# The second matrix product of every tile two slots later, and a new order of the block sums, in a spectral mixing layer with an MLP

## The chip, the cores and the metric

One core of a Trainium2 chip runs the whole program. The metric is device time in microseconds (us) of one execution. Inputs and outputs lie in HBM in float32; matrix products run in float16 with float32 accumulation.

Short names: PE is TensorE (matrix products), PEld its weight loads, DVE is VectorE, ACT is ScalarE, POOL is GpSimd, SP is SyncE, which issues most DMAs. Each of them works through its own queue in order.

## The reference

```python
X = np.fft.rfft(x, axis=1)                    # x: (8, 3008, 256)
Yr = Xr @ w_r - Xi @ w_i + b_r                # 256 x 256 complex mixing
Yi = Xr @ w_i + Xi @ w_r + b_i
Y  = soft-shrink of Yr and Yi by 0.01
y  = np.fft.irfft(Y, n=3008, axis=1)          # (8, 3008, 256)
h  = y.reshape(24064, 256) @ w_in             # w_in: 256 x 2048
out = (s * relu(h)**2 + b) @ w_out            # w_out: 2048 x 256
```

## The kernel before

**Tiles.** The MLP is cut into 48 tiles of up to 512 tokens, numbered 0 to 47 here. Batches 0 and 1 have six "wide" tiles each (0 to 5, 6 to 11), the others five "main" tiles each; the last 14 x 32 tokens of pairs of batches make "tail" tiles of 512 or 384 tokens, put between the batches. Tiles 12, 17, 23, 29, 35 and 41 are the first of batches 2 to 7.

**First stage.** `first_mm(ti, mc)` (L851) is one *slot*: for one of 16 blocks of 128 hidden columns it runs two 128x512 matmuls into half of a two-bank PSUM buffer `psh` (two such buffers). After every odd slot ACT takes the pair out with one relu (`rt`, L871), and either ACT (L881) or DVE (L884) squares it into `gt` (float16). A tile has two `gt` buffers of 8 blocks, q = 0 and q = 1; four of them are in rotation.

**Second stage.** `gt` times `w_out` comes in two forms, both cut into 16 slots of matmuls. `second_mms(ti)` (L922) is the plain form: 64 matmuls of 256 columns into the PSUM banks `psa`, whose results DVE takes out with a scale and a bias (L945). `seven_mms(ti)` (L983) is a Strassen-like form with seven products instead of eight on 2x2 blocks, 112 matmuls of 128 columns, seven in a slot. It is used for tiles 4 to 6, for the last two full tiles ahead of each of the batches 2 to 7 (10, 11, 15, 16, 21, 22, 27, 33, 34, 39) and for 41, 42, 43 and 45. Its blocks of `gt` are called a11, a12, a21, a22, and it needs four operations per half q, all written by `s_op(ti, n, q)` (L965):

- n=1 (DVE, L980): s1 = a21 + a22. 
- n=3 (DVE, L980): a21 = a11 - a21, in place, after n=1.
- n=2 (DVE, L980): a11 = a11 - s1, in place, when product 0 of that half has read a11.
- n=4 (a DMA on POOL's queue that adds, L973): a12 += a11, when product 1 has read a12.

Products 0 and 1 share one PSUM bank, product 2 has the next, 3 and 4 the one after, 5 and 6 the last; outside of the last batch there are two such banks, so product 3 (the matmuls `psa<-T_s,s` in the profile, matmul number 48 of the 112, in slot 6) can't begin until DVE has read products 0 and 1. DVE reads them in `leave(0)` (two adds at L1012, written in slot 4). `leave(1)`, `leave(2)` and `leave(3)` (slots 6, 11 and 15) take the other products out, and `leave(3)` also issues the stores of the tile.

**The work beside it.** A dictionary `plan` puts units of the spectral part at slots, counted over all tiles (`ti * 16 + mc`): `s1_units` (first DFT step, `psf<-x,A_t`, result `u`), `s23_units` (forward step `psf<-F_t,us`, evicted into `xf`, whose two halves DVE sums at L672; the sums' product `psf<-W_t,xf`; the mixing `psf<-W_g,xf`, which DVE adds into `ring` at L699, followed by the shrink at L714 to L716; the inverse step `psf<-ring,T_t`, evicted into `v`), and `s4_units` (last DFT step `psf<-C_t,vs`, evicted into `yt`). They share two PSUM banks, `psf`. `s4_units` of a batch run in the last tile ahead of it (5, 11, 16, 22, 28, 34, 40); `s23_units` of the next batch begin with its first tile (6, 12, 17, 23, 29, 35).

**What sets the order.** The main loop (L1126 on) goes through the tiles and slots: the planned units of the slot, then `first_mm`, then one slot of the second stage of the tile before. In slots 10 and 11 of a seven-product tile it writes the sums n=1 and n=3 of the half q = 0 between `first_mm` and the second stage. Two things stand between the loop and the queues. `evac` and `act_first` choose ACT or DVE for each eviction and each square by running totals of the two engines' planned load, which PE's planned time brings up to date. And the layer that records the kernel orders the instructions of each engine once more by its own model of what is ready, so that neighbours can change places.

The lines of the second stage's plan:

```python
for at, n, q in ((2, 2, 0), (2, 1, 1), (2, 4, 0), (3, 3, 1), (4, 2, 1), (5, 4, 1)):   # L1060
    at += alone and at > 3                     # alone: the last batch
    slots[at].append(lambda n=n, q=q: s_op(ti, n, q))
for at, group in ((4 + alone, 0), (6, 1), (11, 2), (15, 3)):
    slots[at].append(lambda group=group: leave(group))
```

Of the kernel before, what the change touches and what calls it, by code (L numbers as in the profile page):

```python
# [96 lines left out]
def kernel(  # L97
# [19 lines left out]
    MC = DFF // P  # L117
# [694 lines left out]
    def width(tl):  # L812
        return 16 * tl[3] if tl[0] == "wide" else tl[3]
# [37 lines left out]
    def first_mm(ti, mc):  # L851
        tl = tiles[ti]
        w = width(tl)
        if mc % 2 == 0:
            hold_h["ps"] = two_banks()
        ps = hold_h["ps"]
        for dc in range(DC):
            o = ps[:, mc % 2, 0:w]
            r = rhs_of(tl, dc)
            if tl[0] == "main":  # L860
                o = o.rearrange("p (n m) -> p n m", m=16)
            if tl[0] == "wide":
                o = o.rearrange("p (n m) -> p n m", n=HW)
            matmul(
                o, w_in_t[dc][:, mc * P : (mc + 1) * P], r,
                start=(dc == 0), stop=(dc == DC - 1),
            )
        if mc % 2 == 0:
            return
        rt = rpool.tile([P, 2, 512], F32, name="rt", tag="rt")  # L870
        nc.scalar.activation(out=rt[:, :, 0:w], in_=ps[:, :, 0:w], func=AF.Relu)  # L871
        q, g = divmod(mc // 2, 4)
        if g == 0:
            gts[(ti, q)] = gpool.tile([P, 2, 2, 4, 2 * P], F16, name="gt", tag="gt")
        gt = gt_view(ti, q)[g]
        rr = rt[:, :, 0:w]
        if halves(ti):
            rr = rr.rearrange("p k (i t) -> p k i t", i=2)
        work("act", 0.07 + w / 600.0)
        if act_first(pe["now"], 0.09 + w / 600.0, 0.07 + w / 480.0):  # L880
            nc.scalar.activation(out=gt, in_=rr, func=AF.Square)  # L881
            work("act", 0.09 + w / 600.0)
        else:
            last_square[0] = nc.vector.tensor_tensor(out=gt, in0=rr, in1=rr, op=ALU.mult)  # L884
            work("dve", 0.07 + w / 480.0)
# [36 lines left out]
    def second_mms(ti):  # L922

        tl = tiles[ti]
        size = sub_size(tl)
        nsub = -(-tl[3] * (16 if tl[0] == "wide" else 1) // size)
        hold = {}

        def mm(sub, mc):

            alone = ti == len(tiles) - 1 and sub >= 2
            h = 0 if alone else sub % 2
            if h == 0 and mc == 0:
                hold["ps"] = sum_bank(ti).rearrange("p (h e) -> p h e", h=2)
            ps = hold["ps"]
            matmul(
                ps[0:size, h, :],
                lhs_of(ti, mc, sub),
                w_out_t[:, mc, :],
                start=(mc == 0), stop=(mc == MC - 1),  # L940
            )
            if mc == MC - 1 and (alone or h == 1 or sub == nsub - 1):
                k = h + 1
                ost = opool.tile([P, 2, D], F32, name="ost", tag="ost")
                nc.vector.scalar_tensor_tensor(  # L945
                    out=ost[0:size, 0:k], in0=ps[0:size, 0:k], scalar=s_bc[0:size],
                    in1=bias_bc[0:size].unsqueeze(1).to_broadcast([size, k, D]), op0=ALU.mult, op1=ALU.add,
                )
                work("dve", 0.13 + 0.27 * k)
                for i in range(k):  # L950
                    store(tl, sub - k + 1 + i, ost[:, i, :])

        units = [lambda s=s, m=m: mm(s, m) for s in range(nsub) for m in range(MC)]
        per_slot = -(-len(units) // MC)
        return [units[i * per_slot : (i + 1) * per_slot] for i in range(MC)]
# [27 lines left out]
    def seven_mms(ti):  # L983
# [73 lines left out]
        slots = [[] for _ in range(MC)]  # L1057
        for at, what in enumerate(order):
            slots[at // 7].append(lambda w=what: mm(*w))
        for at, n, q in ((2, 2, 0), (2, 1, 1), (2, 4, 0), (3, 3, 1), (4, 2, 1), (5, 4, 1)):  # L1060
            at += alone and at > 3
            slots[at].append(lambda n=n, q=q: s_op(ti, n, q))
        for at, group in ((4 + alone, 0), (6, 1), (11, 2), (15, 3)):
# [3 lines left out]
    def seven(ti):  # L1067
        if ti >= len(tiles) - 2 or not halves(ti):
            return False
        firsts = [mark[b] // MC for b in range(2, B)]  # L1070
        return (
            ti >= firsts[-1] or 4 <= ti < 7 or any(m - 2 <= ti < m for m in firsts)
        )

    plan = {}
# [32 lines left out]
    for b in range(2, B):  # L1108
        s0, s1, s2 = mark[b - 2], mark[b - 1], mark[b]
        p = s1 - s0  # L1110
        units, take_rows = s1_units(b)
# [4 lines left out]
        units, take_half = s23_units(b)  # L1116
# [7 lines left out]
                )  # L1124

    ti_n = len(tiles)  # L1126
    for ti in range(ti_n + 1):
        nxt = [[]] * MC
        if ti:
            nxt = seven_mms(ti - 1) if seven(ti - 1) else second_mms(ti - 1)  # L1130
        for mc in range(MC):
            if ti < ti_n:
                for u in plan.pop(ti * MC + mc, []):
                    u()
                first_mm(ti, mc)
                if mc in (10, 11) and seven(ti):
                    s_op(ti, 1 if mc == 10 else 3, 0)
            for u in nxt[mc]:
                u()
    assert not plan  # L1140


# [28 lines left out]
```

## Time and profile before

| | |
|---|---|
| median of 3 runs | 838.71 us (838.18 to 838.87) |
| the profiled execution | 838.19 us, its span 836.4 us |
| PE busy | 824.2 us, 99% of the span, 7470 matmuls |
| PE weight loads busy | 598.7 us, 72% |
| DVE busy | 698.8 us, 84%, 1061 instructions |
| ACT busy | 712.2 us, 85%, 953 instructions |
| POOL busy | 79.8 us, 10% |
| granted TensorE clock | 1.000 (mean) |
| DMA | 126 GB/s on average |

The span runs from the first to the last instruction of the profiled execution; 1.8 us of its time lie outside of the span. A busy share says how much of the span an engine had an instruction in work. The views used below are the groups of instructions with what ended the idle time ahead of them, the table of who waited for whom, and the timeline, whose rows give start, duration, engine, line, operation, what is written and read, shapes and count. The duration of a row covers the start-up of an instruction too; neighbours overlap a little, so the step from one start to the next is what an instruction costs its queue.

### The profile page before, as it was taken

Reading aid. Unit: us, or ns where it says so; the run is one execution under the profiler, and the core shown is the slowest. Engines: PE = TensorE matmul, PEld = TensorE weight load, DVE = VectorE, ACT = ScalarE, POOL = GpSimd, SP = SyncE. Lnnn points to the kernel's source line nnn. Section 1 sums busy time; section 2 is a strip of 40 time slices with the busy share of each in tenths; the row PEclk is TensorE's granted clock in tenths of the full one; section 3 lists DMA queues with packets and bytes.
Section 4 is the critical chain, followed back from the end, with each engine's and each line's share of the span. In section 5 each row is a group of like instructions: output and inputs, shape, how many; then the busy total and the mean of one; then the engine's idle time right before and its main releaser. Section 6 shows DMA issues by size and latency. Waiting matters only on the chain.

```text
span 836.4 us, 19090 instructions
## 1 busy us (share of the span) xinstructions
PE 824.2 (99%) x7470; PEld 598.7 (72%) x7470; DVE 698.8 (84%) x1061; ACT 712.2 (85%) x953; POOL 79.8 (10%) x106
## 2 busy tenths in 40 slices
PE   8999999999999999999999999999999999999997
PEld 7857767777677767777677776777767777767765
DVE  5988989978898888877888788787889878889885
ACT  5998988998899989988899888988879888788882
POOL 4550001100011001100010000100001000001000
PEclk9999999999999999999999999999999999999999
DMA  8954578345873378534772258713565133513321
GB/s 201 183 150 103 120 181 213 64 96 132 199 185 65 98 181 198 126 88 116 192 190 65 81 131 206 180 47 97 127 177 138 48 97 90 140 45 76 72 66 61
DMA packets 115516, 105.04 MB, mean 126 GB/s; under 512 B 12646, under 2 KB 100714, under 8 KB 114082
## 3 DMA queue, kind: packets, MB, share of 16 engines
q1 hardware_dynamic: 102498, 80.55, 34.0%
q0 software_dynamic: 12928, 23.27, 17.6%
q8 instruction: 58, 0.95, 0.5%
q14 instruction: 32, 0.26, 0.1%
HBM read 53.52 MB, written 46.66 MB: 120 GB/s over the span
## 4 chain that ended last, share of the span: by engine, by line
PE 81%; DVE 8%; ACT 5%; DMA 3%; issue 2%; POOL 0%; SPq 0%; DVEq 0%; ACTq 0%; POOLq 0%
PE psh L175 33%; PE psa L175 30%; PE psf L175 17%; ACT rt L871 2%; DVE gt L884 2%; DVE gt L980 1%; DMA ring<-ring 1%; DMA x<-in_x_dram 1%; PE psm L175 1%; ACT gt L881 1%; DVE s L980 1%; DVE ost L1012 1%; ACT u L187 1%; DMA vd<-v 0%; DVE zz L1012 0%
## 5 line engine op out<-in xcount | busy, mean ns | idle before, releaser
L871 ACT ACTIVATE rt<-psh 128x1024 f32<-128x1024 f32 (+2 forms) x384 | 387.0, 1009 | 67.4 <-PE psh L175 65.2
L175 PEld LDWEIGHTS <-gt 128*128 128x128 f16 (+1 forms) x3568 | 303.7, 101 | 171.1 <-DVE gt L884 0.5
L175 PE MATMUL psh<-yt,w_in 128*128 128x512 f16 (+1 forms) x1344 | 396.5, 378 | 0.1
L884 DVE TENSOR_TENSOR gt<-rt 128x1024 f16<-128x1024 f32 (+2 forms) x254 | 304.9, 1204 | 88.6 <-ACT rt L871 86.8
L175 PE MATMUL psa<-w_out_t,gt 128*128 128x256 f16 (+3 forms) x2512 | 333.1, 258 | 0.0
L175 PEld LDWEIGHTS <-w_in 128*128 128x128 f16 x1536 | 137.3, 98 | 25.9 <-issue 3.2
L881 ACT ACTIVATE gt<-rt 128x1024 f16<-128x1024 f32 (+2 forms) x130 | 134.8, 1037 | 3.2
L187 ACT CAST u<-psf 96x512 f16<-96x512 f32 x96 | 55.7, 581 | 9.3 <-PE psf L175 8.6
L175 PE MATMUL psa<-T_s,gt 128*128 128x128 f16 (+1 forms) x752 | 63.5, 219 | 0.0
L699 DVE TENSOR_TENSOR ring<-psf,s 128x512 f16<-128x512 f32 x84 | 57.6, 685 | 4.2 <-PE psf L175 3.1
L187 ACT CAST v<-psf 128x512 f16<-128x512 f32 x82 | 47.5, 582 | 14.2 <-PE psf L175 13.3
L973 POOL DMA_DIRECT2D gt<-gt x34 | 31.1, 916 | 262.3 <-PE psh L175 86.3
L234 POOL DMA_DIRECT2D x<-in_x_dram x36 | 19.3, 540 | 386.3 <-PE psf L175 337.7
L175 PEld LDWEIGHTS <-xf 128*128 128x128 f16 x504 | 47.4, 98 | 7.2 <-DVE xf L672 1.7
L175 PE MATMUL psh<-tail,w_in 128*128 128x512 f16 (+1 forms) x192 | 52.1, 352 | 0.0
L175 PE MATMUL psf<-W_g,xf 128*128 128x256 f16 x336 | 50.4, 272 | 0.0
L945 DVE SCALAR_TENSOR_TENSOR ost<-psa,s_bc,bias_bc 128x512 f32<-128x512 f32 (+2 forms) x59 | 43.0, 730 | 4.5 <-PE psa L175 2.3
L187 ACT CAST yt<-psf 128x470 f16<-128x470 f32 (+2 forms) x84 | 43.2, 534 | 3.4 <-PE psf L175 2.2
L187 ACT CAST xf<-psf 128x512 f16<-128x512 f32 x67 | 39.1, 584 | 4.3 <-PE psf L175 4.1
L175 PE MATMUL psf<-x,A_t 94*96 94x512 f16 x102 | 38.9, 382 | 1.7 <-ACT yt L187 0.3
L175 PE MATMUL psf<-C_t,vs 96*128 96x94 f16 (+1 forms) x484 | 37.9, 205 | 0.0
L1012 DVE SCALAR_TENSOR_TENSOR ost<-psa,s_bc,zz 128x256 f32<-128x256 f32 (+1 forms) x64 | 28.8, 479 | 5.4 <-PE psa L175 3.6
(118 smaller groups left out, 758.2 us busy)
## 6 DMA issues: line engine op xcount, KB each, us to landing
out_dram<-ost SPq DMA_DIRECT2D x152, 128.0 KB
ud<-u SPq DMA_DIRECT2D x56, 192.0 KB
us<-ud SPq DMA_DIRECT2D x28, 384.0 KB
vd<-v SPq DMA_DIRECT2D x42, 256.0 KB
vs<-vd SPq DMA_DIRECT2D x14, 768.0 KB
x<-in_x_dram POOLq DMA_DIRECT2D x28, 376.0 KB, 6.5
ring<-ring SPq DMA_DIRECT2D x280, 32.0 KB
gt<-gt POOLq DMA_DIRECT2D x30, 256.0 KB, 4.6
```

The costliest lines, as they stand in the source:

```text
L175: return nc.tensor.matmul(out, lhs, rhs, **how)
L187: return None, nc.scalar.copy(out=dst, in_=src)
L234: nc.gpsimd.dma_start(out=t[0:N1, i * w : (i + 1) * w], in_=xv[:, c * XCH * D + i * w : c * XCH * D + (i + 1) * w],)
L699: nc.vector.tensor_tensor(out=ring[0][:, i % 4], in0=ps, in1=hold[i // 2][:, i % 2].unsqueeze(1).to_broadcast([P, 2, D]), op=ALU.add,)
L871: nc.scalar.activation(out=rt[:, :, 0:w], in_=ps[:, :, 0:w], func=AF.Relu)
L881: nc.scalar.activation(out=gt, in_=rr, func=AF.Square)
L884: last_square[0] = nc.vector.tensor_tensor(out=gt, in0=rr, in1=rr, op=ALU.mult)
L945: nc.vector.scalar_tensor_tensor(out=ost[0:size, 0:k], in0=ps[0:size, 0:k], scalar=s_bc[0:size], in1=bias_bc[0:size].unsqueeze(1).to_broad ...
L973: nc.gpsimd.dma_start(out=a12, in_=a11, accum_op=ALU.add)
L980: nc.vector.tensor_tensor(out=out, in0=a, in1=b, op=op)
L1012: nc.vector.scalar_tensor_tensor(out=out, in0=of, scalar=s_bc[0:size], in1=other, op0=ALU.mult, op1=ALU.add)
```

## The change

The second stage of a tile is written two slots later against the first stages: its 16 slots now lie in slots 2 to 15 of the next tile and slots 0 and 1 of the one after. All that is written with it moves along: the plain form's evictions, `leave(0)` to `leave(3)`, the stores and the adding DMAs. The planned spectral units keep their places. The sums n=1 and n=3 of q = 0 move from slots 10 and 11 to slots 12 and 13, and are written behind the second stage's matmuls of the slot instead of ahead of them.

Within the second stage of a seven-product tile, n=1 of q = 1 moves from slot 2 to slot 1, n=3 of q = 1 from slot 3 to slot 2, ahead of n=2 of q = 0, which stays in slot 2. The other sums, the adding DMAs and the four `leave` groups keep their slots relative to the matmuls.

No matmul, weight load, sum or transfer is added or removed by the diff itself.

```diff
-        for at, n, q in ((2, 2, 0), (2, 1, 1), (2, 4, 0), (3, 3, 1), (4, 2, 1), (5, 4, 1)):
+        for at, n, q in ((1, 1, 1), (2, 3, 1), (2, 2, 0), (2, 4, 0), (4, 2, 1), (5, 4, 1)):
...
     ti_n = len(tiles)
-    for ti in range(ti_n + 1):
-        nxt = [[]] * MC
-        if ti:
-            nxt = seven_mms(ti - 1) if seven(ti - 1) else second_mms(ti - 1)
-        for mc in range(MC):
-            if ti < ti_n:
-                for u in plan.pop(ti * MC + mc, []):
-                    u()
-                first_mm(ti, mc)
-                if mc in (10, 11) and seven(ti):
-                    s_op(ti, 1 if mc == 10 else 3, 0)
-            for u in nxt[mc]:
+    LAG = 2
+    behind = {}
+    for at in range((ti_n + 1) * MC + LAG):
+        ti, mc = divmod(at, MC)
+        if ti < ti_n:
+            for u in plan.pop(at, []):
                 u()
+            first_mm(ti, mc)
+        if 0 < ti <= ti_n and mc == 0:
+            mms = seven_mms(ti - 1) if seven(ti - 1) else second_mms(ti - 1)
+            for k, units in enumerate(mms):
+                behind[at + LAG + k] = units
+        for u in behind.pop(at, []):
+            u()
+        if ti < ti_n and mc in (12, 13) and seven(ti):
+            s_op(ti, 1 if mc == 12 else 3, 0)
+    assert not behind
     assert not plan
```

## The prediction

> **What bounds the kernel now.** I read the page's busy times first, then who waited for whom, then the timeline around each place where PE's starts leave a hole.
>
> ```profile
> PE 824.2 (99%) x7470; PEld 598.7 (72%) x7470; DVE 698.8 (84%) x1061; ACT 712.2 (85%) x953; POOL 79.8 (10%) x106
> ```
>
> PE sets the end. Taking each start-to-start step of PE against the step of the same matmul undisturbed (0.216 us for 512 columns, 0.109 for 256, 0.056 for 128), some 9.1 us lie in holes over 60 ns each behind 46 us, where the first stages begin; 7.9 us of them behind 83 us. A change of order can win or lose only there. The Trainium skill (Perfetto Trace Analysis, Identifying the Most-Contended Engine) calls matmul busy time a bad measure and wants MFU and LDWEIGHTS busy: by its LDWEIGHTS share, 72%, 28% of the span would look open. The gapless starts in the rows here bear out the 99%; no other sentence uses this.
>
> The holes that the change aims at are those ahead of product 3, which needs the bank of products 0 and 1:
>
> ```profile
> PE psa L175 <- DVE ost L1012: 1.4, 4, 0.6
> L175 PE MATMUL psa<-T_s,s 128*128 128x128 f16 x176 | 16.9, 219 | 1.6 <-DVE ost L1012 1.4
> ```
>
> By starts they are seven: 0.39 (tile 5), 0.74 (7), 0.31 (11), 0.19 (22), 0.44 (28), 0.19 (34), 0.44 (40), 2.70 us in all. Tile 40, DVE and then PE:
>
> ```profile
> 721.89 1.22 DVE L884 TENSOR_TENSOR gt<-rt 128x1024 f16<-128x1024 f32 x1
> 723.02 0.68 DVE L980 TENSOR_TENSOR gt<-gt,s 128x1024 f16<-128x1024 f16 x1
> 723.62 0.95 DVE L884 TENSOR_TENSOR gt<-rt 128x768 f16<-128x768 f32 x1
> 724.49 0.68 DVE L980 TENSOR_TENSOR s<-gt 128x1024 f16<-128x1024 f16 x1
> 725.21 0.69 DVE L980 TENSOR_TENSOR gt<-gt 128x1024 f16<-128x1024 f16 x1
> 726.00 0.69 DVE L980 TENSOR_TENSOR gt<-gt,s 128x1024 f16<-128x1024 f16 x1
> 726.61 0.48 DVE L1012 SCALAR_TENSOR_TENSOR zz<-psa,s_bc,bias_bc 128x256 f32<-128x256 f32 x1
> 727.13 0.48 DVE L1012 SCALAR_TENSOR_TENSOR ost<-psa,s_bc,zz 128x256 f32<-128x256 f32 x1
> ```
>
> ```profile
> 726.89 0.50 PE L175 MATMUL psa<-T_s,gt 128*128 128x128 f16 x6
> 727.67 0.23 PE L175 MATMUL psa<-T_s,s 128*128 128x128 f16 x1 [0.28 <-DVE ost L1012]
> ```
>
> DVE goes without a gap from the square of slot 15 to the second add of `leave(0)`; PE follows 0.06 later. Steps to carry on: square 1.14 (0.87 at 384 tokens, 1.07 at 480), sum 0.60, add 0.40 to 0.50, and from other rows 0.67 for L945, 0.60 for L699, 0.21 for L672, 0.56 for a `yt` eviction; on ACT relu then square 1.06, square then relu 0.97.
>
> The second place is the start of a batch, tile 23 (it begins at 437.40):
>
> ```profile
> 438.54 1.23 DVE L884 TENSOR_TENSOR gt<-rt 128x1024 f16<-128x1024 f32 x1
> 439.68 0.48 DVE L1012 SCALAR_TENSOR_TENSOR ost<-psa,s_bc,zz 128x256 f32<-128x256 f32 x1
> ...
> 442.08 0.28 DVE L672 TENSOR_TENSOR xf<-xf 128x256 f16<-128x256 f16 x1
> ```
>
> ```profile
> 441.96 0.85 PE L175 MATMUL psf<-W_t,xf 128*128 128x256 f16 x4
> ```
>
> The four `W_t` matmuls take 0.85 instead of 0.60: 0.24 of waiting for the second `xf` sum. At product 3 there is no hole here.
>
> The third is ACT in tile 25, where `v` waits behind a square and holds a `psf` bank; PE loses 0.28:
>
> ```profile
> 473.51 1.02 ACT L871 ACTIVATE rt<-psh 128x1024 f32<-128x1024 f32 x1 [0.96 <-PE psh L175]
> 474.57 1.06 ACT L881 ACTIVATE gt<-rt 128x1024 f16<-128x1024 f32 x1
> 475.53 0.57 ACT L187 CAST v<-psf 128x512 f16<-128x512 f32 x1
> ```
>
> **The change part by part.** It adds no matmul. What counts is the built order of the queues (before and after), which I laid beside these durations.
>
> *(a) Product 3 in the tiles with the last DFT step.* Before, the chain on DVE from the square of slot 15 starts some 0.85 us after the tile, when its relu is out. The built order of after has: that square, n=1, square of slot 1, L945 (which moved here with the second stage), square of slot 3 (in tiles 22, 28, 34, 40 it went from ACT to DVE), n=3, n=2 of q = 0, a `yt` eviction, n=2 of q = 1, two adds. Full tiles (16, 22, 34): 1.14+0.60+0.67+1.14+1.14+3x0.60+0.56+0.51+0.48+0.06 = 8.10, ready at 8.97. PE now gets there two slots later: 6.97 (measured, tile 22) plus two slots of 0.43+0.44+0.21, 9.12: no wait, 0.38 won in 22 and 34. Tile 11 likewise (8.77 against 8.89): 0.31 won. Tiles 28 and 40: chain 7.66, ready 8.50, PE at 6.23+1.94 = 8.17: 0.33 left of 0.44, 0.22 won together. Tile 5 has two slots without DFT units: ready 8.77, PE 8.25: 0.52 instead of 0.39, 0.13 lost. Sum -0.78. So two slots more time are mostly eaten by one more square and L945 in the same stretch.
>
> *(b) Tiles 19, 25, 31.* With more load planned on ACT, the square of slot 1 goes to DVE, which has 2.8 us idle there; `v` leaves right behind the relu. Three holes of 0.28 go: -0.85.
>
> *(c) The first tiles of the batches (6, 12, 17, 23, 35).* Here the lag costs. The square of slot 15 goes to ACT (built order: relu, square), and n=1 of q = 1 needs it, yet stands in DVE's queue ahead of `leave(3)`'s adds (now in slot 1), the square of slot 1 and both `xf` sums. Tile 23, from its start: relu of slot 15 -0.2 to 0.85, its square to 1.95, n=1 2.0 to 2.6, add 3.0, square of slot 1 (its relu came behind that square, out at 2.9) to 4.1, two adds 5.0, `xf` sums out at 5.3 and 5.5. DVE idles 1.7 us ahead of n=1. PE wants `W_t` at 4.56, and 0.22 later by a first-stage matmul that the built order puts ahead: a wait of 0.56 instead of 0.24. Same for 35 (+0.32) and 17 (0.18 and 0.10 of holes before: +0.28); tile 12: 0.68 instead of 0.38 (+0.30); tile 6: 0.48 instead of none. Sum +1.70.
>
> Then product 3 in the same tiles: the built order has, between `leave(0)`'s two adds, the L699 add of the mixing product of slot 8, written when product 3 is about to begin. DVE cannot start it before those `W_g` matmuls are through. Tile 23 from `W_t`'s end (443.18 by the above): square of slot 5 ready 446.04, `xf` 446.25, first add 446.7, L699 447.3, second add 447.8; PE, with four `F_t` and two first-stage matmuls put ahead, comes at 447.5: 0.25 to 0.35, I take 0.25 in 17, 23, 35; tile 6 has one matmul less ahead: 0.50; tile 12 has no L699 between: 0. Sum +1.25.
>
> Tile 7, where both stand in one queue with a shrink: `F_t` of slot 4 waits 0.77 for the bank that L699 empties late, later 0.3 more, against 0.74: +0.36.
>
> *(d) Both ends.* Tile 0 already runs without a second stage; two more such slots make `psh` wait about 0.13 for a relu. At the end the last tile has 18 slots of second stage alone, and the 0.19 hole at 826.6 may go. Together 0, within -0.2 and +0.5 (half a relu).
>
> *(e) Moved for nothing, by cover.* Stores and adding DMAs keep their order on SP and POOL. The second adding DMA of a tile lands 3.4 to 4.8 us after issue, some 3 us ahead of product 6, before and after; without this cover its excess would be PE's wait. In tile 24 the 12 tail stores (7.1 us of issuing on SP) stand ahead of the 8 `ring` DMAs (5.9 us) as before; `leave(3)` is ready at about 458.4, when SP falls free at 458.8. Squares of the plain tiles get two slots more, where PE waits for none today: nothing. The other holes (tiles 2, 3, 8, 14, 15: about 3 us) have queues changed in small ways: 0, from -1 to +1.
>
> Sum: -0.78 - 0.85 + 1.70 + 1.25 + 0.36 + 0 = +1.7 us. On the profiled execution: span 836.4 to 838.1, time 838.19 to 839.9. The median of the runs is 0.5 above that execution: 838.7 + 1.7 = **840.4 us**. About 0.2% (1.7 us) is what a measurement of this kernel can tell from no change, so the forecast, slower, lies at that edge.
>
> **The rivals.**
> *R1, the reordering covers it.* The recording layer already moved matmuls ahead of the waits in (c). If these, or a DVE a little faster than my steps, hide product 3's wait (1.25) and half of `W_t`'s (0.85): -0.4, 838.3. For it: DVE idles 16% of the span. Against: in tiles 7 and 12 before, where such moves stand too, 0.74 and 0.38 stayed.
> *R2, faster.* One mechanism: the head of DVE's queue in tiles 6, 12, 17, 23, 35. If the square on ACT is out by 1.4 us after the tile's start instead of 1.95 (ACT free half a us earlier, relu at once), the sums reach PE in time, the old `W_t` holes go too (0.38+0.28+0.24+0.24), and DVE is early enough at product 3. Then -0.78 + 0.36 - 0.85 - 1.14 = -2.4: 836.3. Against it: the relu can't begin ahead of its matmuls.
> *R3, the delay travels.* `leave(3)` late by 0.5 us or more in the five tiles pushes the stores, and behind them on SP the `ring` DMAs, until `T_t` waits: five times 0.5 on top, 842.9. For it: SP's queue is full there (13 us of issues in a row). Against: `ring` has several slots of slack.
> *R4, it does not do what it says:* the recording order undoes the shift and all holes stay: 838.7. The built order, with `leave(0)` two slots later, speaks against it.
>
> **How the numbers follow.** Chances: forecast 0.46, R1 0.20, R2 0.22, R3 0.10, R4 0.02. The forecast's own range is 839.3 to 842.2 (bounds of d, e and of the 0.25); 0.14 of its 0.46 falls under 0.2%. Faster 0.22 (R2); same 0.14 + 0.20 + 0.02 = 0.36; slower 0.32 + 0.10 = 0.42. The range reaches into R2 and R3 until 0.2 is left out: 836.5 to 843.0.
>
> **What would show it.** Right: holes at `T_s,s` gone in 11, 22, 34, smaller in 28 and 40; none at `x,A_t` in 19, 25, 31; in 17, 23, 35 DVE idle over 1.5 us ahead of the first L980, `W_t` waiting some 0.5 and `T_s,s` 0.2 to 0.4; DVE busy up by about 10 us, ACT down by about 8 (14 squares went to DVE, 16 evictions to ACT and 2 to DVE by the built order). Wrong: `W_t` in tile 23 gapless (R2), or `T_t` waiting for `ring` DMAs (R3).

## The result and the profile after

The changed kernel takes 846.38 us (median of 4 runs, 846.07 to 849.36) against 838.44 us for the kernel before in the same runs (837.61 to 838.87): a ratio of the means of 1.0104, with a 95% interval from 1.008 to 1.0128. By the medians it is 7.9 us slower. The forecast was slower by 1.7 us, 840.4 us, with a range up to 843.0; the time lies above the range.

The profiled execution of after takes 846.14 us with a span of 844.4 us, 8.0 us more than before. The busy times of the page:

```profile
PE 826.7 (98%) x7470; PEld 600.1 (71%) x7470; DVE 707.1 (84%) x1061; ACT 705.3 (84%) x953; POOL 81.3 (10%) x106
```

DVE has 8.3 us more work and ACT 6.9 us less (forecast: about 10 and 8); PE has 2.5 us more busy time for the same 7470 matmuls, and its clock is granted at 0.996 on average instead of 1.000 (half of that loss is one stretch in the first 12 us, ahead of the first stages; the other is told below). The table of who waited for whom, PE's rows behind 46 us that matter (total us, times, longest):

```profile
PE psf L175 <- DMA vs<-vd: 3.5, 3, 2.2
...
PE psf L175 <- DVE xf L672: 1.3, 4, 0.4
PE psa L175 <- DVE ost L1012: 1.2, 3, 0.5
PE psa L175 <- DMA gt<-gt: 1.1, 2, 0.8
```

Two of these rows are waits for transfers, `vs<-vd` and the adding DMA `gt<-gt`. Before, this table has neither behind 125 us. The chain that ended last says the same: by engine, in the kernel before

```profile
PE 81%; DVE 8%; ACT 5%; DMA 3%; issue 2%; POOL 0%; SPq 0%; DVEq 0%; ACTq 0%; POOLq 0%
```

and after:

```profile
PE 74%; DMA 11%; DVE 8%; ACT 4%; issue 2%; SPq 1%; POOL 0%; DVEq 0%; POOLq 0%; ACTq 0%
```

Measured as in the prediction, by PE's start-to-start steps over the undisturbed step, the holes add up to 20.8 us before and 28.75 us after, all the 8 us of the span. By the matmul that waits (us; places that hardly differ are left out; the last three columns are experiments told below):

| PE waits at | before | after | loads held | and small adds | before, three edits |
|---|---|---|---|---|---|
| `C_t` (mostly for `vs`) | 0.18 | 4.53 | 0.83 | 1.54 | 1.20 |
| half clock, no wait | 0 | 1.65 | 0 | 0 | 0 |
| product 6 (adding DMA) | 0 | 1.40 | 2.79 | 0 | 0 |
| product 3 (`T_s,s`) | 2.70 | 2.62 | 2.63 | 2.60 | 1.86 |
| `W_t` (`xf` sums) | 1.12 | 2.31 | 2.31 | 2.30 | 1.02 |
| `x,A_t` (`v` eviction) | 2.61 | 1.71 | 1.71 | 1.70 | 1.77 |
| `F_t`, `ring` | 1.36 | 1.36 | 1.35 | 1.53 | 1.31 |
| first 46 us | 9.56 | 9.96 | 10.00 | 9.92 | 9.63 |
| all holes | 20.8 | 28.75 | 24.81 | 22.72 | 20.35 |

The first three rows are new but for 0.18 us and hold 7.4 of the 8.0 us. The row of the first 46 us is not the change's doing: the first 559 matmuls, up to 54 us, stand in the same order in both kernels, and profiles of kernels without the lag differ there by up to 1.7 us. The rows that the prediction worked out are compared with it further below.

**Where `vs` goes late.** SP writes `v` out to the buffer `vd` in HBM (L744) and fetches it back in another layout as `vs` (L755), which `C_t` needs; `u` goes by `ud` to `us` in the same way. SP's queue at the last `vd` write of tile 21, before:

```profile
406.90 1.27 SPq L899 DMA_DIRECT2D out_dram<-ost  x2
409.20 0.38 SPq L744 DMA_DIRECT2D vd<-v  x1
...
411.63 0.79 SPq L755 DMA_DIRECT2D vs<-vd  x2
```

and the x load that GpSimd issues there:

```profile
409.62 0.52 POOL L234 DMA_DIRECT2D x<-in_x_dram  x1 [10.98 <-PE psf L175]
```

The stores go out 2.3 us ahead of `vd`, `vd` goes out 0.42 us ahead of the x load, and 2.43 us later it has landed and `vs` is fetched. After, the order on SP is the same, but the times are not:

```profile
414.11 1.27 SPq L899 DMA_DIRECT2D out_dram<-ost  x2
415.48 0.41 SPq L744 DMA_DIRECT2D vd<-v  x1
...
422.53 0.79 SPq L755 DMA_DIRECT2D vs<-vd  x2
```

```profile
414.89 0.52 POOL L234 DMA_DIRECT2D x<-in_x_dram  x1 [10.97 <-PE psf L175]
```

The stores now wait for an eviction of the second stage (L945, 413.33 to 414.08), and `vd`, whose `v` is out at 414.45, stands behind their two issues (1.27 us). It leaves 0.59 us behind the x load and lands 7.05 us later. What the DMA engines carry in these 8 us (415 to 423) by queue, with packets, MB and the share of 16 engines' time:

```profile
q0 software_dynamic: 112, 0.39, 39.9%
q1 hardware_dynamic: 912, 0.72, 28.6%
```

The 112 packets of GpSimd's queue, the x load's, take more of the engines than the 912 packets of SP's: worked out from these rows, one packet of the load has an engine for 0.46 us, one of SP's for 0.04. The Trainium skill (DMA: Bandwidth & Descriptors, Queues, rings and completion order) says that a DMA engine goes round its queues and serves a whole packet of one before the next; `vd`'s small packets taking turns with the load's large ones would agree with these rows, but no view shows single packets waiting. The same happens in tiles 10 and 27 (8.6 and 6.9 us from `vd` to `vs`, 3.7 and 2.4 before), and PE waits in slot 0 of the next tiles: 2.40 us in tile 11, 0.67 in 22, 0.94 in 28. The longest, on PE's timeline:

```profile
232.37 0.60 PE L175 MATMUL psa<-w_out_t,gt 128*128 128x256 f16 x4
235.21 0.38 PE L175 MATMUL psf<-C_t,vs 96*128 96x94 f16 x5 [2.23 <-DMA vs<-vd]
```

**And what the hole does to the clock.** Busy time in stretches around it, with the granted clock, the DMA share and GB/s in the last columns:

```profile
232.00:236.00 4.00, 1.77 (x17) 1.03 (x15) 1.97 (x3) 1.18 (x2) 0.07 (x1) 1.00 1.03 260
236.00:240.00 4.00, 4.00 (x34) 2.97 (x33) 2.81 (x4) 2.55 (x5) 0.00 (x0) 0.57 0.94 240
```

From 236.4 to 239.8 us PE runs at half clock: matmuls of 480 columns step by 0.40 instead of 0.20. That costs another 1.65 us, for which no row of the waits answers.

**The places that the prediction worked out.** Tile 40, DVE and then PE:

```profile
733.63 1.29 DVE L980 TENSOR_TENSOR gt<-gt,s 128x1024 f16<-128x1024 f16 x2
734.83 0.64 DVE L189 CAST yt<-psf 128x470 f16<-128x470 f32 x1
735.39 0.47 DVE L1012 SCALAR_TENSOR_TENSOR zz<-psa,s_bc,bias_bc 128x256 f32<-128x256 f32 x1
735.90 0.48 DVE L1012 SCALAR_TENSOR_TENSOR ost<-psa,s_bc,zz 128x256 f32<-128x256 f32 x1
```

```profile
735.52 0.37 PE L175 MATMUL psf<-C_t,vs 96*128 96x94 f16 x5
...
736.06 0.50 PE L175 MATMUL psa<-T_s,gt 128*128 128x128 f16 x6
736.44 0.23 PE L175 MATMUL psa<-T_s,s 128*128 128x128 f16 x1
```

DVE's queue is the forecast one, `yt` ahead of the adds. Product 3 no longer waits; 0.28 us of the old 0.44 are now lost at the `C_t` matmul ahead of it (735.52), whose bank the same `yt` eviction empties. Tile 23, DVE and then PE:

```profile
443.95 1.22 DVE L884 TENSOR_TENSOR gt<-rt 128x1024 f16<-128x1024 f32 x1
445.27 0.69 DVE L980 TENSOR_TENSOR s<-gt 128x1024 f16<-128x1024 f16 x1
...
448.19 0.48 DVE L672 TENSOR_TENSOR xf<-xf 128x256 f16<-128x256 f16 x2
...
452.46 0.68 DVE L699 TENSOR_TENSOR ring<-psf,s 128x512 f16<-128x512 f32 x1
453.06 0.47 DVE L1012 SCALAR_TENSOR_TENSOR ost<-psa,s_bc,zz 128x256 f32<-128x256 f32 x1
```

```profile
448.53 0.61 PE L175 MATMUL psf<-W_t,xf 128*128 128x256 f16 x4 [0.30 <-DVE xf L672]
...
453.59 0.62 PE L175 MATMUL psa<-T_s,s 128*128 128x128 f16 x8
```

Tile 23 begins at 443.29: the sum n=1 starts 1.98 us in (forecast 2.0), `W_t` is held 0.46 us (forecast 0.56), and L699 stands ahead of the second add, so that product 3 is held 0.28 us (forecast 0.25). What n=1 stands behind is not the forecast picture, though. The square of slot 15 is on ACT, as forecast:

```profile
443.10 1.02 ACT L871 ACTIVATE rt<-psh 128x1024 f32<-128x1024 f32 x1 [0.35 <-PE psh L175]
444.16 1.06 ACT L881 ACTIVATE gt<-rt 128x1024 f16<-128x1024 f32 x1
```

It ends at 445.21. But DVE does not stand idle for it: it squares slot 13 until 445.16 (the first of the DVE rows above) and has 0.1 us of idle time ahead of n=1, where step (c) had 1.7. Tiles 17 and 35 show the same; ahead of n=1 DVE idles 0.18 us in tile 12 and 0.58 in tile 6. ACT in tile 25:

```profile
479.83 1.02 ACT L871 ACTIVATE rt<-psh 128x1024 f32<-128x1024 f32 x1 [0.96 <-PE psh L175]
481.30 0.59 ACT L187 CAST v<-psf 128x512 f16<-128x512 f32 x1 [0.44 <-PE psf L175]
```

The square between the two is gone from ACT, `v` waits for PE alone, and the hole of 0.28 us is gone.

### The profile page after: what moved, and what is told of

The parts are those of the page before. It is cut to its first block, busy times and chain, and to the rows that moved or that the text cites. A ratio compares the mean times of both kernels' runs of the same rounds, so it can differ in the third digit from the quotient of the medians.

```text
span 844.4 us, 19096 instructions
## 1 busy us (share of the span) xinstructions
PE 826.7 (98%) x7470; PEld 600.1 (71%) x7470; DVE 707.1 (84%) x1061; ACT 705.3 (84%) x953; POOL 81.3 (10%) x106
## 4 chain that ended last, share of the span: by engine, by line
PE 74%; DMA 11%; DVE 8%; ACT 4%; issue 2%; SPq 1%; POOL 0%; DVEq 0%; POOLq 0%; ACTq 0%
PE psh L175 30%; PE psa L175 27%; PE psf L175 16%; DMA vd<-v 3%; DMA vs<-vd 2%; DVE gt L884 2%; DMA gt<-gt 2%; ACT rt L871 2%; DMA ring<-ring 1%; DMA out_dram<-ost 1%; DMA x<-in_x_dram 1%; DVE ost L1012 1%; PE psm L175 1%; DVE ring L699 1%; DMA us<-ud 1%
## 5 line engine op out<-in xcount | busy, mean ns | idle before, releaser
L884 DVE TENSOR_TENSOR gt<-rt 128x1024 f16<-128x1024 f32 (+2 forms) x268 | 321.7, 1205 | 75.2 <-ACT rt L871 75.0
L881 ACT ACTIVATE gt<-rt 128x1024 f16<-128x1024 f32 (+2 forms) x116 | 120.2, 1036 | 2.7
L699 DVE TENSOR_TENSOR ring<-psf,s 128x512 f16<-128x512 f32 x84 | 57.6, 686 | 11.7 <-PE psf L175 10.3
L187 ACT CAST yt<-psf 128x470 f16<-128x470 f32 (+2 forms) x89 | 44.9, 518 | 10.6 <-PE psf L175 9.0
L945 DVE SCALAR_TENSOR_TENSOR ost<-psa,s_bc,bias_bc 128x512 f32<-128x512 f32 (+2 forms) x59 | 43.0, 729 | 8.2 <-PE psa L175 7.9
L187 ACT CAST xf<-psf 128x512 f16<-128x512 f32 x75 | 43.5, 585 | 4.3 <-PE psf L175 4.1
```

Of the source, the lines that this page charges most:

```text
L187: return None, nc.scalar.copy(out=dst, in_=src)
L699: nc.vector.tensor_tensor(out=ring[0][:, i % 4], in0=ps, in1=hold[i // 2][:, i % 2].unsqueeze(1).to_broadcast([P, 2, D]), op=ALU.add,)
L945: nc.vector.scalar_tensor_tensor(out=ost[0:size, 0:k], in0=ps[0:size, 0:k], scalar=s_bc[0:size], in1=bias_bc[0:size].unsqueeze(1).to_broad ...
```

## The experiments

Theory D: the loss is the late last `vd` write, which shares the DMA engines with the x load, so that `vs` comes late. Its rivals: the order of the sums, the lateness of the stores by itself, the DVE queue at the start of a batch, and the adding DMAs. All times are medians of the runs, each beside runs of the kernel before on the same chip (838.5 to 838.9 us).

**The two parts of the change.** The lag alone, with the sums in their old order:

```diff
-        for at, n, q in ((1, 1, 1), (2, 3, 1), (2, 2, 0), (2, 4, 0), (4, 2, 1), (5, 4, 1)):
+        for at, n, q in ((2, 2, 0), (2, 1, 1), (2, 4, 0), (3, 3, 1), (4, 2, 1), (5, 4, 1)):
```

> The lag of two slots alone, the sums of the seven-product tiles in their old order. Theory D (the loss is in the DMA queues: with the lag, the stores of a plain tile go ahead of the last write of vd on SP, that write then shares the DMA engines with the load of the next x, and the last DFT step waits for vs): the same loss as the full change, 845 to 847 us against 838.4, holes ahead of psf<-C_t,vs in slot 0 of tiles 11, 22 and 28. Theory Q (the loss is in DVE's queue at the start of a batch, by the new order of the sums): 840 to 842 us, as the first sum no longer stands so early. Theory S (the new order of the sums is good and hides part of the loss): slower than the full change, 847 to 849.

It takes 845.82 us (843.42 to 849.06), ratio 1.0089 [1.0058, 1.0121]. The other half, the new order of the sums put into the kernel before (the same line the other way round, without the lag):

> The new order of the sums alone, without the lag. Theory D: no loss, 837 to 839 us; no waits for vs; the holes ahead of product 3 (2.7 us in all before) shrink a little, as the first two sums can run while products 0 and 1 are in work, and the x DFT step's holes in tiles 19, 25 and 31 stay. Theory Q: 840 to 841, as n=1 of q = 1 stands ahead of the xf sums here too.

It takes 840.78 us (839.02 to 843.19), ratio 1.0022 [1.001, 1.0034]. The lag carries the loss: with it alone, `vd` to `vs` takes 8.5, 7.1 and 7.0 us in tiles 10, 21 and 27 and the `C_t` holes are 4.84 us. The sums by themselves cost about 2 us, as theory Q had it and not theory D: `W_t` waits 1.97 us instead of 1.12 and product 3 3.10 instead of 2.70. With the lag the order of the sums makes no difference there (`W_t` 2.29 us in the old order, 2.31 in the new).

**Late stores, without the lag.** Before, with each store written two slots later and everything else in place:

```diff
-                    store(tl, sub - k + 1 + i, ost[:, i, :])
+                    put_off(tl, sub - k + 1 + i, ost[:, i, :])
...
+            for what in due.pop(slot[0], []):
+                store(*what)
```

> The kernel before with every store of the output written two slots later and nothing else moved; PE's queue is the same matmul for matmul. Theory D: this alone brings most of the loss, since the stores now stand ahead of the last vd write on SP: that write lands 7 to 9 us after its issue instead of 2.4 to 3.7, holes ahead of psf<-C_t,vs in tiles 11, 22 and 28 of 2 to 4 us in all, with a clock at half for 3.4 us if one of them is over 2 us; 841 to 845 us. Theory Q: no difference, 838 to 839.

It takes 838.87 us (837.25 to 842.23), ratio 1.0003 [0.9989, 1.0016], and `vd` to `vs` stays at 2.35 to 3.8 us in these tiles. But the edit did not make the stores late where it matters. SP's queue in tile 21:

```profile
408.56 1.27 SPq L899 DMA_DIRECT2D out_dram<-ost  x2
410.87 0.38 SPq L744 DMA_DIRECT2D vd<-v  x1
```

Both rows stand 1.7 us later than in the kernel before, as everything does there (1.7 us are lost in the first 46 us of this profile): the order is that of before, the stores go out when their data are ready, and `vd` follows 2.3 us behind them and 0.42 us ahead of the x load. The same holds in tiles 10 and 27. So this run is no test of theory D; the kernels that follow are.

**Stores behind `vd`, with the lag.** After, with the stores one slot later still and held behind the last `vd` write on SP:

```diff
+        with ExitStack() as order_of:
+            if last_vd:
+                order_of.enter_context(tc.issue_after(last_vd[0].ins))
+            for what in due.pop(at, []):
+                store(*what)
```

> The changed kernel with every store written one slot later and held behind the last vd write on SP. Theory D: the vd writes of the tiles 10, 21 and 27 go out 1.3 us earlier and land in 2.4 to 4 us; the holes ahead of psf<-C_t,vs (4.0 us) and the slow clock behind the one of 2.4 us (1.7 us) go: 840 to 841 us. Theory Q: nothing of the loss goes, 845 to 847.

It takes 842.79 us (840.67 to 844.63), ratio 1.0046 [1.0028, 1.0065]: 3.6 us come back, if not all that was expected. `vd` leaves 0.42 us ahead of the x load again, `vd` to `vs` falls to 2.42, 2.4 and 2.4 us, the `C_t` holes to 0.81. But the waits at product 6 grow to 2.99 us, a second transfer that the profile of after only hinted at.

**The x load held, with the lag.** After, with the three loads of the collisions held until the first half of `vs` has landed, by a one-element copy on GpSimd; SP's queue stays as it is:

```diff
-                    lambda b=b, c=c: emit_load_x(b + 1, chunks=range(c, c + 1))
+                    lambda b=b, c=c: emit_load_x(
+                        b + 1,
+                        vs[(b - 1, 0)][0:1, 0, 0:1] if c == 1 and b in (3, 5, 6) else None,
+                        range(c, c + 1),
+                    )
```

> After, with the three x loads that run at the ends of tiles 10, 21 and 27 (chunk 1 of batches 4, 6 and 7) held back until the first half of vs has landed (a 1-element copy on GpSimd waits for it). Nothing else changes: stores still stand ahead of the last vd write, the lag is 2. Theory D (the late vd write shares the DMA engines with the x load's 4 KB packets, so vs lands late and C_t holds PE): vd to vs falls from 7 to 8.6 us to 2.4 to 4 us, the C_t holes from 4.5 us to under 0.8, the clock stays at 1.0: 840 to 842.5 us. Rival (the stores ahead of vd, or SP's own issuing, make vs late): vd to vs stays at 6 us or more and the time at 845 or above.

It takes 842.29 us (841.32 to 844.33), ratio 1.005 [1.0034, 1.0065]: 4.1 us come back. SP's queue in tile 21:

```profile
410.36 1.27 SPq L899 DMA_DIRECT2D out_dram<-ost  x2
411.73 0.41 SPq L744 DMA_DIRECT2D vd<-v  x1
...
415.50 0.79 SPq L755 DMA_DIRECT2D vs<-vd  x2
```

`vd` is as close behind the stores as in after (1.37 us), but without the load beside it lands in 3.77 us instead of 7.05. The half clock is gone too. So the load beside `vd` is most of the delay, 3.3 of 4.6 us. The other 1.3 us, up from the 2.43 of before, remain with the stores right ahead; in tile 33 of after, where no x load runs, `vd` to `vs` takes 3.61 us instead of 2.45 in the same way. What is left of the waits:

```profile
PE psa L175 <- DMA gt<-gt: 2.2, 3, 1.0
PE psf L175 <- DVE xf L672: 1.3, 4, 0.4
PE psa L175 <- DVE ost L1012: 1.2, 3, 0.5
```

**The collision in the kernel before.** No lag; the last `vd` write of the same three batches is held behind the next `ud` write on SP:

```diff
+            def write_behind():
+                with tc.issue_after(last_ud[0].ins):
+                    write()
...
+            if i == H - 1 and b in (2, 4, 5):
+                plan.setdefault(mark[b] - 28, []).insert(0, write_behind)
```

> Before (no lag, old sums), with the last vd write of batches 2, 4 and 5 held behind the next ud write on SP, so that it goes out some 1 us later, behind the x load instead of ahead of it. Theory D: vd to vs grows from 2.4 to 3.7 us to 6 to 8.6 us, C_t waits in slot 0 of tiles 11, 22 and 28 for 2 to 4.5 us in all: 841 to 843.5 us. Rival (it takes the lag's other effects, 1 us of delay alone is covered): under 0.5 us of C_t holes and 838.4 to 839.3 us.

It takes 839.25 us (838.57 to 840.61), ratio 1.0011 [1.0002, 1.0021]. SP's queue in tile 10, where the x load goes out at 219.26:

```profile
219.97 1.22 SPq L745 DMA_DIRECT2D vd<-v  x1
227.96 0.30 SPq L765 DMA_DIRECT2D vs<-vd  x1
```

The mechanism is there without any lag: 8.0 us from `vd` to `vs` instead of 3.7 (5.4 and 5.5 in tiles 21 and 27), and PE is held 1.93 us in tile 11. The price was expected too high, 2 to 4.5 us; the time, 0.7 us more, lies where the rival had it. In tiles 22 and 28 PE does not wait for `vs`: `vd` lands in 5.4 to 5.5 us there instead of the 7 us of after. Of the three collisions, one costs. So the collision by itself makes a smaller loss than in after.

**Half the lag.** After with a lag of one slot:

```diff
-    LAG = 2
+    LAG = 1
...
-        if ti < ti_n and mc in (12, 13) and seven(ti):
-            s_op(ti, 1 if mc == 12 else 3, 0)
+        if ti < ti_n and mc in (11, 12) and seven(ti):
+            s_op(ti, 1 if mc == 11 else 3, 0)
```

> After with a lag of one slot instead of two (sums of the first half in slots 11 and 12). Theory D has a threshold: with one slot less the stores are out before the last v is, vd leaves ahead of the x load as in before, no C_t hole above 0.3 us, no half clock: 838 to 840.5 us. Rival (the loss grows with the lag, slot by slot): half of it, 842 to 843 us, with C_t holes of about 2 us.

It takes 852.44 us (850.45 to 855.31), ratio 1.0169 [1.0142, 1.0197]: both expectations miss, it is the slowest of all. With one slot the plan puts DVE's work in yet another order, and product 3 waits 8.35 us instead of 2.62. On the disputed point: `vd` leaves at 415.31 in tile 21, 0.23 us behind the x load (415.08), and takes 6.3 us; the `C_t` holes are 1.83 us. `vd` meets the load already at one slot of lag; if there is a threshold, as theory D has it, it lies below that.

**The start of a batch.** Two tries at step (c), both on top of the held loads (842.29 us). First, the square of slot 15 ahead of a batch on DVE instead of ACT:

```diff
-        if act_first(pe["now"], 0.09 + w / 600.0, 0.07 + w / 480.0):
+        to_dve = mc == MC - 1 and ti in (5, 11, 16, 22, 34)
+        if not to_dve and act_first(pe["now"], 0.09 + w / 600.0, 0.07 + w / 480.0):
```

> The kernel with the x loads held back (the first of this set), and besides the square of slot 15 in tiles 5, 11, 16, 22 and 34 put on DVE instead of ACT. By step (c) of the prediction n=1 of q=1 then needn't wait for relu and square in turn on ACT: the W_t holes of tiles 12, 17, 23 and 35 fall from 2.0 us to under 1.2, and those at product 3 in 17, 23 and 35 (0.28 each), where L699 now stands behind both adds, go: 1.2 to 2 us below the first of this set, 838.5 to 841 us. Rival (these squares only move the queue, ACT or DVE pays elsewhere): within 0.5 us of the first of this set.

It takes 848.26 us (843.95 to 849.84): 6 us more instead of 1.2 to 2 less. The product 3 holes fall to 1.69 us as worked out, but `W_t`'s rise to 5.07. DVE had no idle time to fill: in tile 23 it now runs the squares of slots 13 and 15 one after the other (444.08 to 446.44) ahead of n=1, where after has one, and the n=3 sum besides stands between the two `xf` sums. At tile 6 the second adding DMA holds product 6 for 2.59 us, with half clock behind it. Second, n=1 of q = 1 behind the two `xf` sums:

```diff
+            if (n, q) == (1, 1) and ti in (5, 11, 16, 22, 34):
+                order_of.enter_context(tc.issue_after(last_xf[0].ins))
             nc.vector.tensor_tensor(out=out, in0=a, in1=b, op=op)
```

> The kernel with the three x loads held behind vs (842.3 us), and n=1 of q=1 in tiles 5, 11, 16, 22 and 34 (its second stage runs in the first tile of a batch) put behind the two xf sums in DVE's queue. By step (c) DVE no longer stands 1.7 us idle for n=1: the W_t holes of tiles 12, 17, 23 and 35 fall from 2.0 us to under 0.9, and the time to 840.8 to 841.8 us. Rival (the later sums reach product 3 or the second adding DMA later and PE pays there): W_t holes gone, but the time within 0.4 us of 842.3 or above.

It takes 842.67 us (841.33 to 846.22), ratio 1.0049 [1.0033, 1.0066]; the rival holds. `W_t` waits 1.26 us in all instead of 2.31, and product 3 waits 4.24 instead of 2.63. Whichever of the two stands first in DVE's queue, PE waits for the other, as one would expect of a queue that has no 1.7 us of idle time to win.

**The adding DMAs.** With the held loads, product 6 still waits 2.8 us. First the old order of the sums, so that the first adding DMA goes out ahead of the second again:

> The kernel with the three x loads held behind vs (842.3 us), and the old order of the sums, so that the first adding DMA of a tile goes out well ahead of the second again. Theory A (with the new sums both adding DMAs go out within a microsecond or two of each other and share the engines, the second lands late, and product 6 holds PE 2.8 us): the waits at product 6 fall to under 1 us and the time to 839.8 to 841.2 us. Rival (they land late because the lag moves them beside the us loads, whatever their order): 2 us or more stay, 841.8 us or above.

It takes 843.08 us (841.83 to 845.14), ratio 1.0049 [1.0034, 1.0063]. The waits at product 6 fall by half, to 1.50 us, but the time does not: theory A misses. In this profile the waits at `F_t` and `ring` are 2.18 us instead of 1.35, and all holes together fall by 0.3 us only. Then the transfer itself, cut to a sixteenth of its bytes, with every engine's queue unchanged, with the lag and the held loads, and for comparison in the kernel before (the rest of `a12` stays without its term, so the output is not the layer's):

```diff
-            nc.gpsimd.dma_start(out=a12, in_=a11, accum_op=ALU.add)
+            nc.gpsimd.dma_start(out=a12[0:8], in_=a11[0:8], accum_op=ALU.add)
```

> The lagged kernel with the three x loads held behind vs (842.3 us), its adding DMAs cut to 8 of the 128 partitions (the other 120 rows of a12 stay without a11, so product 6 and the output are not the reference's there). Every engine's queue is the same. Theory (product 6 waits for the second adding DMA, and these bytes crowd the others): no wait at product 6, 839 to 840.2 us, 2.1 to 3.3 us less. Rival (product 6 only stands where another wait comes next, on DVE or a psf bank, or the sums are late themselves): less than 1 us gained, 841.3 us or above.

> Before, with the same cut of the adding DMAs, and the same queues as before. Its profile has no wait at product 6, so by the theory it gains nothing: 838.0 to 838.9 us. If it gains 1 us or more, these DMAs cost before too, by crowding others, and the gain of the lagged kernel is only in part the lag's.

With the lag it takes 840.12 us (839.13 to 841.86), ratio 1.0014 [0.9999, 1.0028], 2.2 us less than with the whole transfer; product 6 doesn't wait at all. Before, it takes 837.97 us (837.53 to 840.43), ratio 0.9995 [0.9984, 1.0007]: no gain that can be told. So the adding DMAs are covered in the kernel before and not with the lag. How they go out in tile 28, before:

```profile
526.77 0.91 POOL L973 DMA_DIRECT2D gt<-gt  x1 [3.25 <-PE psh L175]
529.67 0.87 POOL L973 DMA_DIRECT2D gt<-gt  x1 [1.99 <-PE psf L175]
```

and with the lag and the held loads, and the wait at product 6 that follows:

```profile
532.11 1.80 POOL L973 DMA_DIRECT2D gt<-gt  x2 [6.99 <-PE psh L175]
```

```profile
541.20 0.23 PE L175 MATMUL psa<-w_out_t,gt 128*128 128x128 f16 x1 [0.61 <-DMA gt<-gt]
```

Before, the two leave 2.9 us apart and land 4.6 and 6.1 us after issue; with the lag they leave 0.6 us apart, and the second lands after 8.5 us. By the built order the sum n=2 of q = 0, which the first needs, now stands behind n=1, n=3, L945 and two squares more in DVE's queue.

**What can be had without the lag.** Step (b) alone in the kernel before:

```diff
+        to_dve = mc == 1 and ti in (19, 25, 31)
+        if not to_dve and act_first(pe["now"], 0.09 + w / 600.0, 0.07 + w / 480.0):
```

> Before, with only the square of slot 1 in tiles 19, 25 and 31 put on DVE: step (b) of the prediction alone. v leaves right behind the relu, the three holes of 0.28 us ahead of x,A_t go, nothing else moves: 0.85 us faster than before, 837.3 to 838.0 us. Rival (DVE's ring and xf work behind the square comes later): within 0.3 us of before or slower.

It takes 837.91 us (837.06 to 841.17), ratio 0.9986 [0.9968, 1.0004]. The three holes of 0.28 us are gone; the median is 0.8 us lower, as worked out, though the interval still touches 1, and in tile 40 of this profile product 3 waits 0.79 us instead of 0.44. With it, n=2 of q = 1 behind `leave(0)`'s adds in all seven-product tiles:

```diff
-        for at, n, q in ((2, 2, 0), (2, 1, 1), (2, 4, 0), (3, 3, 1), (4, 2, 1), (5, 4, 1)):
+        for at, n, q in ((2, 2, 0), (2, 1, 1), (2, 4, 0), (3, 3, 1), (5, 2, 1), (5, 4, 1)):
...
+            if (n, q) == (2, 1):
+                order_of.enter_context(tc.issue_after(last_add[0].ins))
```

> Before, with those three squares on DVE, and n=2 of q=1 in every seven-product tile put behind the adds of leave(0) (only product 4 and the second adding DMA need it). Product 3's bank is then free 0.7 us earlier: 2.7 us of holes there fall to under 0.7, the three of 0.28 go, and the second adding DMA goes out 1.5 us later. If it stays covered: 835.3 to 836.3 us. Rival (it was covered by 1 us only, and product 6 waits for it now): 1 us or more of holes at product 6, 837 to 839 us.

It takes 841.34 us (839.8 to 842.9), ratio 1.0031 [1.0019, 1.0042]: slower than either side expected. Product 3 waits 0.79 us instead of 2.70, but product 6 now waits 4.31 us, in tile 28 like this,

```profile
539.77 0.23 PE L175 MATMUL psa<-w_out_t,gt 128*128 128x128 f16 x1 [1.86 <-DMA gt<-gt]
```

and the last tiles wait 2.43 us for the sum itself. With the second adding DMAs 0.9 to 3.1 us further behind the first, some of them are uncovered without any lag. Last, the same two edits, the second in tiles 22, 34 and 40 alone, where no wait at product 6 had shown:

```diff
-            at += alone and at > 3
+            at += alone and at > 3 or (n, q) == (2, 1) and ti in (21, 33, 39)
...
+            if (n, q) == (2, 1) and ti in (21, 33, 39):
+                order_of.enter_context(tc.issue_after(last_add[0].ins))
```

> Before, with the square of slot 1 in tiles 19, 25 and 31 on DVE, and n=2 of q=1 behind the adds of leave(0) in the second stages that run in tiles 22, 34 and 40 alone, where the run with all tiles showed no wait at product 6. Three holes of 0.28 and the product 3 holes of these tiles (0.19, 0.19, 0.44) go: 1.66 us below before, 836.5 to 837.4 us. Rival (the later adding DMA reaches product 6 in tile 22 or 34 after all, or the square on DVE costs its 0.3 at tile 40): 837.5 to 838.8 us.

It takes 837.01 us (835.83 to 839.23, 12 runs) against 838.61, ratio 0.9983 [0.9972, 0.9993]: 1.6 us faster, where 1.66 was worked out, and the fastest version of this study. PE's waits behind 125 us:

```profile
PE psa L175 <- DVE ost L1017: 1.1, 3, 0.6
PE psf L175 <- DMA vs<-vd: 1.0, 1, 1.0
```

By PE's starts product 3 has its holes in tiles 5, 7, 11 and 28 alone; those of 22, 34 and 40 are gone. The wait for `vs` is in tile 16, ahead of the matmul where the kernel before has 0.18 us; in this place it differs from profile to profile (0.32 to 0.93 us in four of the other versions of the kernel before).

## Why the prediction was wrong

The direction was right, slower; the size was wrong, 7.9 us instead of 1.7. The step that failed is (e), "Moved for nothing, by cover", which put stores and adding DMAs at nothing; the runs show 7 us of waits for transfers and slow clock there. The right direction owes something to luck: in the places that the forecast worked out the holes grow by 0.7 us only, hardly to be told from no change. Point by point:

- *(a) Product 3 with the last DFT step.* Forecast -0.78, measured -0.87: gone in 11, 22 and 34 (-0.69), 0.12 left in 28 and 0.28 in 40, both at the `C_t` matmul instead of product 3; tile 5 waits 0.57 at product 3 (forecast 0.52) and 0.12 more at a `C_t` matmul ahead of it. Right.
- *(b) `v` in 19, 25, 31.* Forecast and measured -0.85. Right; the three holes went too where this step was made alone in the kernel before.
- *(c) The first tiles of the batches.* `W_t` waits 0.57 in 12 and 0.46 in 17, 23 and 35 (forecast 0.68 and 0.56), product 3 waits 0.28 in 17, 23 and 35 (0.25), 0.69 in 6 (0.50) and 0.10 in 12 (0). Tile 6 has no `W_t` wait (0.48 forecast), tile 7 lost 0.08 instead of 0.36. In all +2.5 instead of +3.3: right in place, 0.8 us too high. One reading behind it is wrong: "DVE idles 1.7 us ahead of n=1" is 0.1 us in tiles 17, 23 and 35, as DVE still has the square of slot 13 to do. That n=1 begins within 0.02 us of the forecast is partly luck: this square and the one on ACT end within 0.05 us of each other. The two kernels that tried to mend the waits built on that idle time, and both failed: DVE's queue is full there, and the wait goes back and forth between `W_t` and product 3.
- *(d) Both ends.* The waits of `psh` in tile 0 are 0.65 us instead of 0.54 (forecast 0.13 more), and the 0.19 at the end is gone: -0.1 in all, forecast 0.
- *(e) Cover.* "Stores and adding DMAs keep their order on SP and POOL" is true and was the wrong test. The order is kept, but the stores at the head of SP's queue now wait for data that come two slots later, and the step did not ask what stands behind them: the last `vd` write, late by 1 us, meets the x load. That is 4.0 us of `C_t` holes in tiles 11, 22 and 28 and 1.65 us of half clock. "The second adding DMA of a tile lands 3.4 to 4.8 us after issue, some 3 us ahead of product 6, before and after" was too short even for the kernel before, whose 17 second adding DMAs land 3.2 to 7.4 us after issue, and took the spacing of the two as fixed; the price is 1.40 us in after, 2.79 once PE is no longer held at `vs`. The order given for tile 24 is a misreading without effect: the 8 `ring` DMAs of 5.9 us go out ahead of the tail stores (452.83 against 458.87), and the 8 behind them take 5.3 us. The bound from -1 to +1 for the other holes was for DVE and ACT only, and left out the transfers.

(a) to (d) together measure +0.7 us by the holes of after, against +1.7; (e)'s places hold 7.1 of the 8.0 us. The experiments agree on where the rest comes from: with the loads held and the adding DMAs cut, the lagged kernel takes 840.12 us, 2.15 us above the kernel before with the same cut. That this is near the forecast difference of 1.7 is partly luck. Of the 1.9 us of holes that this profile has more than that of before, 0.5 is a wait for `vs` in tile 16 and 0.4 lies in the first 46 us, and neither is a term of the forecast.

Of the rivals, R1, R2 and R4 are out: the waits of (c) are there, the kernel is slower, and the holes did move. R3 had the carrier right, stores waiting on SP with others queued behind them, but at another place and with another victim: it took `leave(3)`'s stores and the `ring` DMAs at the starts of batches, 2.5 us; it was L945's stores and `vd` in the plain tiles ahead of them, and the price came for the most part from the x load on the DMA engines, not from waiting in SP's queue. The `ring` holes went from 0.81 to 0.32 us.

What stays open: `vd` takes 5.5 us in tiles 21 and 27 of the kernel before with `vd` held, and 7 in after, at about the same distance behind the load (0.71 and 0.59 us in tile 21). The stores go out 3.4 us ahead of `vd` in the first and 1.4 us ahead in the second, and without a load such close stores cost 1.1 to 1.3 us (above); an estimate from this difference, no run has it alone. Open is also whether the waits at `F_t` and `ring` grow in the old order of the sums because those at product 6 shrink.

## What to carry to other kernels

An unchanged queue order is not an unchanged time: where a change makes an instruction wait longer, go through everything that stands behind it on its queue, DMA issues above all, and look up what the DMA engines carry at the new time. A transfer counts as covered only against its slowest landing in the trace, and with its neighbours where the change puts them, not where they were. Look in the trace that idle time is really there before moving work into it. And a gain that comes from single forecast holes can be had, here 1.6 us with six moves, by moving the instructions that make them without shifting the rest; the same move made in every tile cost 2.7 us.

## What was not expected of the hardware

**Half clock behind a short hole.** PE's granted clock fell to 0.5 for 3.4 us at holes of 2.40 us (after, tile 11), 2.19 us (the lag of one slot, tile 28) and 2.59 us (the squares on DVE, tile 6), between 0.4 us ahead of the hole's end and 1.3 us behind it. In the 17 traces of this case it happens nowhere else between 20 us and the last 5 us of the span. A hole of 2.43 us in the kernel with the lag alone, and of 1.93 us in the one with `vd` held, had no such effect. The Trainium skill (TensorE: Matmul & The Clock Gate, What's actually happening) puts the fall behind at least one idle window of 3413 ns that runs freely. The traces agree on the window and not on its being idle. Within each trace all steps of the clock stand a whole number of 3.41 us apart, and what counts is how much PE idles within one stretch of this grid. The stretch ahead of the fall in after, and the two that share the hole of 2.43 us in the kernel with the lag alone (PE's busy time is the first number behind the length, the granted clock the third from the end):

```profile
233.01:236.42 3.41, 1.21 (x15) 0.96 (x16) 1.74 (x2) 0.80 (x2) 0.00 (x0) 1.00 1.01 255
```

```profile
229.45:232.87 3.42, 2.66 (x19) 1.59 (x17) 2.47 (x3) 1.99 (x3) 0.51 (x1) 1.00 1.00 242
232.87:236.28 3.41, 1.90 (x22) 1.43 (x23) 1.65 (x3) 1.48 (x3) 0.00 (x0) 1.00 1.00 244
```

PE idles 2.20 us in the first, 0.76 and 1.51 in the other two. In the same way, 2.02 us (the lag of one slot) and 2.00 us (the squares on DVE) within one stretch were enough, 1.54 us (`vd` held) and 1.86 us (n=2 of q = 1 behind the adds, in all tiles, at 537.40) were not. So whether a hole of some 2 to 2.5 us costs more than its own length depends here on where the grid cuts it. In the first 20 us, where the matmuls are others, 1.4 us could be enough. Where the clock falls, it costs 1.4 to 1.7 us more.

**Half a microsecond decides over five.** A `vd` write of 256 KB issued 0.42 us ahead of the x load landed in 2.4 us (before, tile 21; 3.7 in tile 10), as fast as in tile 33 with no load; issued 0.23 to 0.71 us behind it, in 5.4 to 8.6 us. By the estimate above, up to 1.3 us of the longer times are the stores right ahead of `vd`.
